# Mixer block on one core: the last query block as two half passes, closing products over 128 rows

## The chip, the cores and the metric

The kernel runs on one core of one Trainium2 chip. The metric is the device time of one execution in microseconds. Engines are named as in the profile: PE multiplies matrices (PEld are its weight loads), DVE and ACT work element by element, POOL too, and SP issues the DMAs.

## What is computed

```python
def reference(A_x, A_wqkv, A_wo, B_x, B_w1, B_b1, B_w2, B_b2):
    xn = layernorm(A_x)                              # 2048 x 640
    q, k, v = split(xn @ A_wqkv)                     # 32 heads of 20
    p = softmax(q @ k.T / sqrt(20))                  # per head, 2048 x 2048
    s = concat_heads(p @ v) @ A_wo                   # attention
    h = layernorm(xn)                                # B_x is not used
    u = gelu(h.T @ B_w1 + B_b1)                      # token MLP, 640 x 1536
    g = silu((u @ B_w2 + B_b2).T)                    # 2048 x 640
    return A_x + s * g
```

All arrays are bf16. The exponentials of the attention, 32 x 2048 x 2048 of them, are most of the work.

## The kernel before

**Passes.** The 32 heads are eight groups of four (`NG`, `GH`), the 2048 queries four blocks of 512 (`NTB`). One pass is one head group with one query block; there are 32 (`passes`, L852 to L855), and the last eight alternate between groups 6 and 7, so that group 7 with query block 3 comes last. A pass has 16 key chunks of 128. A unit is one chunk and one head: a score product of 32 rows by 128 columns with 512 queries as the moving side (`emit_st`, L1206, head g on row group 32g of the array), then exponentials, then a product P·V of 128 rows by 21 columns (20 values and a column of ones for the denominator; `pv_mm`, L1284, head g on column group 32g). All P·V products of a pass add up in PSUM bank 6 (`AB`).

**Two ways for the exponentials.** Most units go to ACT, which takes two or three PSUM banks in one instruction (L1235, 128x1024 or 128x1536). Of the chunks in `RC` some go to DVE: it makes the bit pattern of a power of two from a score (L1246), and of this tile three shifted ones (L1268, one instruction for four heads each); four P·V products with differently scaled values (`v_sb`, `vs_sb`) sum them up. Such a chunk costs DVE 4 + 3 instructions, and PE four P·V products a head.

**The order.** A planner in `schedule` writes the instruction list of every engine when the kernel is built. It keeps a modelled time for each engine and picks, step by step, among ready score groups, P·V groups, the steps of jobs, and fillers (`emit_fill`, L1299, products with zero weights that add nothing), with settings for each 16 units from a fixed table (`PLAN`, `tune`). Each engine runs its own list in order; semaphores carry the waits. In the planner, products on different groups of the array share 216 ns.

**Around the output.** When the last P·V product of a pass is placed, `ep_steps` (L1377) puts the epilogue on DVE: a transpose out of bank 6 (L1400), reciprocals of the denominators, a multiplication, and for groups 6 and 7 a transpose back into `stage_sb`. The results of groups 0 to 5 come back through DRAM into `oT_sb` (which is `xnT_sb`) as chunks 0 to 3, those of groups 6 and 7 as chunk 4. The closing product of a block of 128 queries is five products of `oT_sb` with `wo` (`op_mms`, L929), for 512 output columns and once more for the last 128; then DVE multiplies by the gate (L944) and adds x (L954). For the blocks of query block 3 chunk 4 holds only group 6, 48 rows, and L929 takes just these 48; group 7's share comes from `stage_sb` by one further product (L934).

**The tail.** Blocks 12 to 15 are closed in the tail. `tail_pre` and `tail_pre_b` (the 128-column parts of all four blocks, in bank 7, `JB`, cleared by a product with zeros, L1631) place the products with L929; the epilogue of the last pass is in two halves of 256 queries (L1392 to L1399); `tail_end` adds L934; `tail_fin` multiplies (L1607) and adds (L1609, on POOL for the first two blocks); `tail_b` does the 128-column parts at once (L1623, L1625); four stores (L1616) end it.

Of the kernel before, what the change touches and what calls it, by code (L numbers as in the profile page):

```python
# [6 lines left out]
dt = mybir.dt  # L7
# [3 lines left out]
P = 128  # L11
# [249 lines left out]
class _Kern:  # L261
# [154 lines left out]
    def schedule(self):  # L416
# [437 lines left out]
        passes += [(L6, 0), (L6, 1), (L7, 0), (L7, 1), (L6, 2), (L7, 2), (L6, 3), (L7, 3)]  # L854
        NP = len(passes)  # L855
        pass_of = {gp: q for q, gp in enumerate(passes)}
        UP = NB * GH

# [56 lines left out]

        def reload7_steps(p):
            def make(bk):
                return oT_loads(560, 640, p * 512, 512, [S_(f"oTd{L7}_{p}")], f"oTb_{p}", f"oTl7{p}") + [
                    ("tag", f"oT5_{p}")]
            return make  # L920

        def op_mms(b, ap, c0, n, bslot, first=True, last=True, opens=True, closes=True):
# [3 lines left out]
            if first:  # L926
                for c in range(5):
                    k = 128 if c < 4 or full else 48
                    steps.append(("pe", lambda e, c=c, k=k: e.matmul(  # L929
                        ap, oT_sb[0:k, c, b * 128:(b + 1) * 128], wo_ap[0:k, c, c0:c0 + n], start=(opens and c == 0),  # L930
                        stop=(full and c == 4)),
                        oT_slots.get(("oTa", c), []) + oT_slots.get((f"oTb_{p}", c), []) + [S_("wo")], [bslot], f"op{b}", mm(n)))
# [26 lines left out]
        def store_steps(p):  # L959
            def make(bk):  # L960
                dst = out[0, p * 512:(p + 1) * 512, :].rearrange("(b p) d -> p b d", p=P)
                src = regC[:, p * 4:(p + 1) * 4, :]
                return [("dma", lambda e: e.dma_start(dst, src), [S_(f"res{b}") for b in range(4 * p, 4 * p + 4)], [],
                         f"out{p}", 655360)]
            return make
# [42 lines left out]

        def activate():
            changed = True  # L1010
# [54 lines left out]
        pv_tot = [UP] * NP  # L1065
        pv_left = [UP]
# [6 lines left out]
        def chunk_ok(q, c):  # L1073
            G, p = passes[q]
            return f"qk{G}_1_{c // 4}{kpart(c) if G == 0 else ''}" in done and f"qk{G}_0_{p}" in done

        def next_chunk(q, cl):
            while q < NP:
                free = [c for c in range(NB) if (q, c) not in cl]
                if free:  # L1080
                    nr = [c for c in free if c not in RC]
# [40 lines left out]
        def a_left(q):  # L1122
            n = sum(4 for c in range(NB) if (q, c) not in claimed)
            if a_cur[1] is not None and a_cur[0] == q:
                n += GH - a_cur[2]
            return n

        done_cost = {"pe": 0.0, "dve": 0.0, "act": 0.0}
        def d_claimable():
            if not self.DON:  # L1130
                return None
            if tfree and dlive[0] < self.NLIVE:
# [3 lines left out]
                for q in (q0, q0 + 1):  # L1136
# [5 lines left out]
                    for r, c in enumerate(RC):  # L1142
# [48 lines left out]
        def emit_st(lst, banks):  # L1191
# [6 lines left out]
            for i, (q, c, g) in enumerate(lst):  # L1198
# [3 lines left out]
                lhsT = qk_sb[32 * g:32 * g + 32, slot, 1, c * 128:(c + 1) * 128]  # L1202
                rhs = qk_sb[32 * g:32 * g + 32, slot, 0, p * 512:(p + 1) * 512]
                outp = ps(bk)
                cost = (first if i == 0 else 0.0) + (20.0 if i < n - 1 else tot - 20.0 * (n - 1))
                pr.pe(lambda e, outp=outp, lhsT=lhsT, rhs=rhs, g=g: e.matmul(outp, lhsT, rhs, start=True, stop=True,  # L1206
                                                                            tile_position=(32 * g, 0)),
                      reads=[S_(f"qkb{slot}_0_{p}_{g}"), S_(kslot(slot, c, g))] + ([S_(f"qkp_{g}")] if slot else []), writes=[bank_slot[bk]],
                      name=f"st{q}_{c}_{g}", cost=cost, w=53.0)
# [70 lines left out]
        def pv_mm(q, g, lhsT, rhs, reads, cost, name, last):  # L1280
            k = pv_seen.get((q, g), 0)
            pv_seen[(q, g)] = k + 1
            outp = ps_all[32 * g:32 * g + DH + 1, AB * 512:AB * 512 + 512]
            pr.pe(lambda e: e.matmul(outp, lhsT, rhs, start=(k == 0), stop=last, tile_position=(0, 32 * g)),  # L1284
                  reads=reads, writes=[bank_slot[AB]], name=name, cost=cost, w=53.0)
# [3 lines left out]
        def fill_ok():  # L1289
            q = pv_pass[0]  # L1290
            return (acc_ok[0] and q < NP and all(pv_seen.get((q, g), 0) > 0 and pv_g_left.get((q, g), NB) > 0
                                                 for g in range(4)))

        def emit_fill():
            tot = 216.0 + pe_cost("pv", 0.0)
            for g in range(4):
                outp = ps_all[32 * g:32 * g + DH + 1, AB * 512:AB * 512 + 512]
                rhs = wp_sb[:, 0:2, :, :]
# [14 lines left out]
        def emit_pv(items, quads):  # L1313
# [22 lines left out]
            for g in range(4):  # L1336
                left = pv_g_left.get((q, g), NB) - len(ends) - sum(1 for x in items if x[1][2] == g)
# [3 lines left out]
            for i, s in enumerate(seq):  # L1341
                cost = tot / n
                if s[0] == "d":
                    _, d, k, g = s
                    c, b = d["c"], d["tl"][k]
                    if k == 0:
                        lhsT = v_sb[:, c, G * 4 + g, 0:DH + 1]
                        rd = [S_(f"v{half}_{c}")]
                    else:
                        lhsT = vs_sb[:, G % 2, k - 1, d["r"], g * 22:g * 22 + DH + 1]  # L1350
                        rd = [S_(f"vs{G % 2}_{k - 1}_{d['r']}")]
                    rhs = dt_sb[:, b, g, :].bitcast(bf)
                    pv_mm(q, g, lhsT, rhs, rd + [S_(f"dt{b}_{g}")], cost, f"pvd{q}_{c}_{g}", i in final)
                else:
# [3 lines left out]
                    pv_mm(q, g, v_sb[:, c, G * 4 + g, 0:DH + 1], pt_sb[:, s0, :], [S_(f"pt{s0}"), S_(f"v{half}_{c}")],  # L1358
                          cost, f"pv{q}_{c}_{g}", i in final)
# [7 lines left out]
            if pv_left[0] == 0:  # L1367
                pv_pass[0] += 1
                pv_left[0] = UP
# [7 lines left out]
        def ep_steps(q):  # L1377
            G, p = passes[q]
            last_pass = q == NP - 1
            s_ = q % 2  # L1380
            steps = []
            if last_pass:
                def half(h):
                    a, b = 256 * h, 8 * h
                    din = bass.AP(tr_sb, a, [[512, P], [32, 8]])
                    rd = rden_sb[:, b:b + 8]
                    nin = bass.AP(tr_sb, a + 1, [[512, P], [32, 8], [1, DH]])
                    rin = bass.AP(rden_sb, b, [[16, P], [1, 8], [0, DH]])
                    nout = bass.AP(on_sb, a + 1, [[512, P], [32, 8], [1, DH]])
                    tr, on, rs = S_(f"tr_{h}"), S_(f"on_{h}"), S_(f"rden_{h}")  # L1390
                    return (
                        ("dve", lambda e: e.transpose(tr_sb[:, a:a + 256], ps(AB, 256, a)), [bank_slot[AB]], [tr],  # L1392
                         f"eqT{h}", 366.0),
                        ("dve", lambda e: e.reciprocal(rd, din), [tr], [rs], f"eqr{h}", 110.0),
                        ("dve", lambda e: e.tensor_tensor(nout, nin, rin, ALU.mult), [tr, rs], [on], f"eqm{h}", dv(160)),
                        ("dve", lambda e: e.transpose(stage_sb[:, 2, a:a + 256], on_sb[:, b:b + 8, :].rearrange(
                            "p a b -> p (a b)")), [on], [S_(f"stage2_{h}")], f"eqb{h}", 361.0))
                A, B = half(0), half(1)
                return [A[0], A[1], B[0], A[2], B[1], A[3], ("tag", f"ep{q}_0"), B[2], B[3], ("tag", f"ep{q}_1")]  # L1399
            steps.append(("dve", lambda e: e.transpose(tr_sb[:, :], ps(AB)), [bank_slot[AB]], [S_("tr")], f"epT{q}", 632.0))  # L1400

            def okacc():
                acc_ok[0] = True
            steps.append(("call", okacc))
# [170 lines left out]
        for p in range(NTB - 1):  # L1575
            for b in range(4 * p, 4 * p + 4):
                rq = ("oT", "wo", f"oT5_{p}", f"oT4_{p}", f"x2_{p}", f"a2_{b}")
# [3 lines left out]
            add_job(f"st{p}", store_steps(p), tuple(f"res{b}" for b in range(4 * p, 4 * p + 4)), 30.0)  # L1581

        LB = [NB - 4 + i for i in range(4)]
# [10 lines left out]
        def tail_end(i):  # L1594
            b, bk = LB[i], tbank[i]
            steps = []
            if i == 2:
                for k in range(4):
                    steps += op_mms(LB[k], ps(JB, 128, 128 * k), 512, 128, bank_slot[JB], False, True, False, k == 3)
            steps += op_mms(b, ps(bk), 0, 512, bank_slot[bk], False, True)  # L1600
            steps.append(("tag", f"tend{i}"))
            return steps

        def tail_fin(i):
# [4 lines left out]
            steps.append(("pool" if i < 2 else "dve", lambda e: e.tensor_tensor(g0, g0, regA[:, b, 0:512], ALU.add),  # L1609
                          [S_(f"r{b}_0"), S_(f"x2_{NTB - 1}")], [S_(f"res{b}")], f"tr{b}a",  # L1610
                          1180.0 if i < 2 else dv(512, .52)))
# [7 lines left out]
        def tail_b():  # L1619
            gb = regC[:, NB - 4:NB, 512:640]  # L1620
            xb = regA[:, NB - 4:NB, 512:640]
            pb = ps(JB).rearrange("p (i n) -> p i n", i=4)
            return [("dve", lambda e: e.tensor_tensor(gb, pb, gb, ALU.mult),  # L1623
                     [bank_slot[JB]] + [S_(f"g{b}") for b in LB], [S_("rb")], "tpB", dp(512)),
                    ("dve", lambda e: e.tensor_tensor(gb, gb, xb, ALU.add), [S_("rb"), S_(f"x2_{NTB - 1}")],  # L1625
                     [S_("resb")], "trB", dv(512, .52)), ("tag", "tB")]

        tail_req = ("oT", "wo", f"x2_{NTB - 1}", f"oT4_{NTB - 1}") + tuple(f"a2_{b}" for b in LB)
        for i in range(4):
            add_job(f"tpre{i}", (lambda bk, i=i: tail_pre(i) + [("tag", f"tpre{i}")]), tail_req + (f"tbank{i}",), 60.0, at=NP - 1.9)  # L1630
# [3 lines left out]
        add_job("tpreb", (lambda bk: [zero] + sum((tail_pre_b(i) for i in range(4)), []) + [("tag", "tpreb")]),  # L1634
                tail_req + (f"bankoff{JB}",), 59.0, at=NP - 1.9)
        for i in range(4):
# [375 lines left out]
```

The softmax here doesn't subtract the row's maximum and nothing guards it: scores larger than these inputs give would overflow.

## Time and profile before

| what | us |
|---|---|
| median of 3 runs (lowest, highest) | 755.73 (755.54, 755.74) |
| profiled execution: from the first to the last instruction | 753.7 |
| median less span: what lies around it | 2.07 |
| last exponential starts | 740.76 |
| last P·V product starts | 742.88 |
| last closing product starts (L934) | 749.54 |
| last store is issued | 751.29 |

The profiled execution is one launch; its own time is taken as the span and the 2.07 us around it. Matmuls are shown from their start to a modelled end: a product with 512 moving columns shows 0.38 to 0.39 us even where the next starts 0.216 after it, so starts tell more than durations. DVE and ACT instructions overlap their neighbours a little too: L1246 shows 0.68 and comes every 0.60, the exponential of 1024 columns comes every 0.90 and that of 1536 every 1.33.

### The profile page before, as it was taken

The numbers are of one execution on the slowest core, as the hardware profiler recorded it, in microseconds if no ns is written. First come the engines' busy times: TensorE is split into PE (matmuls) and PEld (weight loads), VectorE is DVE, ScalarE is ACT, GpSimd is POOL, SyncE is SP. The second block draws the span as 40 slices with busy tenths as digits, with TensorE's granted clock in tenths as the row PEclk, the third lists the DMA queues.
The fourth block names the chain that finished last, engine by engine and source line by source line (L and its number), as shares of the span: only waits on it lengthen the run. The fifth ranks groups of instructions, "written<-read, shape, count | busy, mean of one in ns | idle before, by whom it ended". The sixth has DMA issues, their size and how long they took to land.

```text
span 753.7 us, 23158 instructions
## 1 busy us (share of the span) xinstructions
PE 717.6 (95%) x10302; PEld 240.7 (32%) x10302; DVE 721.0 (96%) x1320; ACT 729.9 (97%) x695; POOL 15.6 (2%) x22
## 2 busy tenths in 40 slices
PE   9999999999999999999999999999999988998997
PEld 7432223222323232323223323233333232222222
DVE  8869999999999999999999999999999999999997
ACT  4999999999999999999999999999999999999993
POOL 4200000000000000000000000000000000000001
PEclk9999999999999999999999999999999999999999
DMA  9584111110313031121014022223124340011011
GB/s 245 109 167 57 38 26 38 20 36 7 86 14 77 13 68 38 35 61 21 7 37 111 26 49 52 47 54 102 44 57 82 76 150 11 6 47 48 13 47 36
DMA packets 117143, 42.54 MB, mean 56 GB/s; under 512 B 75300, under 2 KB 115876, under 8 KB 116996
## 3 DMA queue, kind: packets, MB, share of 16 engines
q1 hardware_dynamic: 117044, 41.07, 23.9%
q8 instruction: 80, 1.31, 0.7%
q14 instruction: 19, 0.16, 0.1%
HBM read 26.37 MB, written 10.22 MB: 49 GB/s over the span
## 4 chain that ended last, share of the span: by engine, by line
ACT 85%; PE 12%; DVE 2%; DMA 1%; issue 0%; POOL 0%
ACT pt_sb L1235 83%; PE ps_all L1284 4%; PE ps_all L644 4%; PE ps_all L1206 4%; ACT zt_sb L840 1%; ACT zt_sb L835 1%; PE ps_all L929 1%; DMA xnT_sb<-regC 1%; DVE bst_sb L531 0%; DVE bst_sb L533 0%; DMA regA<-in_A_x_dram 0%; DVE regC L549 0%; DVE regC L1607 0%; PE ps_all L683 0%; DVE xnT_sb L611 0%
## 5 line engine op out<-in xcount | busy, mean ns | idle before, releaser
L1235 ACT ACTIVATE pt_sb<-ps_all 128x1024 bf16<-128x1024 f32 (+1 forms) x672 | 710.5, 1226 | 2.4 <-PE ps_all L1206 1.9
L1246 DVE TENSOR_SCALAR dt_sb<-ps_all 128x512 uint16<-128x512 f32 x496 | 328.2, 684 | 10.1 <-PE ps_all L1206 8.3
L1206 PE MATMUL ps_all<-qk_sb 32*128 32x512 bf16 x2048 | 266.7, 384 | 27.7 <-ACT pt_sb L1235 24.8
L1268 DVE TENSOR_SCALAR dt_sb<-dt_sb 128x2048 uint16<-128x2048 uint16 x372 | 241.9, 687 | 1.4
L1206 PEld LDWEIGHTS ps_all<-qk_sb 32*128 32x128 bf16 x2048 | 67.0, 91 | 283.8 <-ACT pt_sb L1235 231.8
L1284 PE MATMUL ps_all<-dt_sb,vs_sb 128*21 128x512 bf16 x1488 | 124.6, 382 | 0.8 <-DVE dt_sb L1268 0.7
L1284 PE MATMUL ps_all<-pt_sb,v_sb 128*21 128x512 bf16 x1552 | 124.2, 382 | 0.9 <-DVE tr_sb L1400 0.6
L644 PE MATMUL ps_all<-regB,regA 128*32 128x128 bf16 (+1 forms) x1536 | 68.2, 301 | 0.7 <-DVE regB L845 0.3
L644 PE MATMUL ps_all<-regC,regA 128*32 128x512 bf16 (+1 forms) x1536 | 68.4, 301 | 0.0
L1284 PE MATMUL ps_all<-dt_sb,v_sb 128*21 128x512 bf16 x496 | 49.0, 384 | 0.3 <-DVE tr_sb L1400 0.2
L644 PE MATMUL ps_all<-xnT_sb,wqk_sb 128*32 128x512 bf16 x640 | 48.2, 382 | 0.3 <-DVE zt_sb L814 0.2
L1284 PEld LDWEIGHTS ps_all<-dt_sb,vs_sb 128*21 128x21 bf16 x1488 | 31.5, 91 | 41.3 <-issue 21.9
L1284 PEld LDWEIGHTS ps_all<-pt_sb,v_sb 128*21 128x21 bf16 x1552 | 28.7, 90 | 47.7 <-issue 38.0
L644 PEld LDWEIGHTS ps_all<-regB,regA 128*32 128x32 bf16 x1536 | 27.2, 96 | 27.0 <-issue 13.1
L644 PEld LDWEIGHTS ps_all<-regC,regA 128*32 128x32 bf16 x1536 | 27.3, 96 | 25.6 <-issue 13.4
L929 PE MATMUL ps_all<-wv_sb,xnT_sb 128*128 128x128 bf16 (+3 forms) x160 | 29.5, 302 | 0.1
L644 PE MATMUL ps_all<-wv_sb,xnT_sb 128*32 128x480 bf16 x320 | 23.0, 369 | 0.0
L1400 DVE STREAM_TRANSPOSE tr_sb<-ps_all 128x512 f32<-128x512 f32 x31 | 22.1, 711 | 0.9 <-PE ps_all L1284 0.7
L644 PEld LDWEIGHTS ps_all<-xnT_sb,wqk_sb 128*32 128x32 bf16 x640 | 13.7, 95 | 18.2 <-issue 7.7
L1284 PEld LDWEIGHTS ps_all<-dt_sb,v_sb 128*21 128x21 bf16 x496 | 12.6, 90 | 21.3 <-issue 14.7
L814 DVE TENSOR_SCALAR zt_sb<-ps_all,b2h_sb 128x512 bf16<-128x512 f32 (+1 forms) x32 | 17.2, 544 | 0.0
L1044 DVE CAST v_sb<-ps_all 128x480 bf16<-128x480 f32 (+1 forms) x22 | 13.4, 610 | 3.3 <-PE ps_all L737 3.1
(82 smaller groups left out, 307.0 us busy)
## 6 DMA issues: line engine op xcount, KB each, us to landing
regA<-in_B_w_dram SPq DMA_DIRECT2D x6, 1024.0 KB
regA<-in_B_w_dram SPq DMA_DIRECT2D x8, 768.0 KB
qk_sb<-qk_scratch_dram SPq DMA_DIRECT2D x56, 80.0 KB
qk_scratch_dram<-qs_sb SPq DMA_DIRECT2D x32, 128.0 KB
regA<-in_A_x_dram SPq DMA_DIRECT2D x6, 640.0 KB
ok_scratch_dram<-on_sb SPq DMA_DIRECT2D x96, 20.0 KB
out_dram<-regC SPq DMA_DIRECT2D x3, 640.0 KB
wqk_sb<-in_A_wqkv_dram SPq DMA_DIRECT2D x2, 480.0 KB
```

The source lines that it names most:

```text
L644: fns.append(lambda e, c=c, e_=e_: e.matmul(oc(c, e_), lhsT[:, c:e_], rhs, start=start, stop=stop, tile_position=(0, c)))
L814: steps.append(("dve", lambda e, z=z, i=i, jj=jj: e.tensor_scalar(z[:, c0:c0 + n], ps(bk, n, i * n), 0.5, bias[:, jj:jj + 1], ALU.mult, AL ...
L835: steps.append(("act", lambda e: e.activation(tt_, tt_, AF.Tanh, scale=1.5957691216), [stt], [stt], f"th{j}", ac(n)))
L840: steps.append(("act", lambda e: e.activation(tt_, z, AF.Tanh), sz, [stt], f"th2_{j}", ac(n)))
L929: steps.append(("pe", lambda e, c=c, k=k: e.matmul(ap, oT_sb[0:k, c, b * 128:(b + 1) * 128], wo_ap[0:k, c, c0:c0 + n], start=(opens and c ...
L1044: return lambda e: e.tensor_copy(dst, src)
L1206: pr.pe(lambda e, outp=outp, lhsT=lhsT, rhs=rhs, g=g: e.matmul(outp, lhsT, rhs, start=True, stop=True, tile_position=(32 * g, 0)), reads=[ ...
L1235: tk = pr.act(lambda e: e.activation(outp, inp, AF.Exp, scale=math.log(2.0) / 128.0), reads=[bank_slot[b] for b in banks[:n]], writes=[S_( ...
L1246: tk = pr.dve(lambda e: e.tensor_scalar(w, src, WOFF, 0.0, ALU.add, ALU.max), reads=[bank_slot[bk]], writes=[S_(f"dt{d['tl'][0]}_{g}")], n ...
L1268: tk = pr.dve(lambda e: e.tensor_scalar(dst, src, dk, None, ALU.add), reads=[S_(f"dt{b0}_{g}") for g in range(4)], writes=[S_(f"dt{b}_{g}" ...
L1284: pr.pe(lambda e: e.matmul(outp, lhsT, rhs, start=(k == 0), stop=last, tile_position=(0, 32 * g)), reads=reads, writes=[bank_slot[AB]], na ...
L1400: steps.append(("dve", lambda e: e.transpose(tr_sb[:, :], ps(AB)), [bank_slot[AB]], [S_("tr")], f"epT{q}", 632.0))
```

## The change

The last pass, group 7 with query block 3, becomes two consecutive passes of 256 queries (`HALF`). A unit of such a pass is a pair of key chunks with one head (`HP`): two score products of 256 queries, side by side in one PSUM bank, so that ACT and DVE still see 512 columns, and two P·V products of 256 queries, one after the other into the same 256 columns of bank 6. A half pass has eight units a head instead of 16. The two chunk pairs (2, 5) and (8, 11) may go to DVE. `NP` is 33; the number of units is as before, and so is the table of settings. The planner prices each of the two products at half of what one was.

Each half pass has its own epilogue of 256 queries. Blocks 12 and 13 become ordinary closing jobs that wait for the epilogue of the first half (with the product with `stage_sb` in them), and have one store. Blocks 14 and 15 alone stay for the tail; the order of its products is changed a little, and only the first block's add is on POOL. `op_mms` always takes all 128 rows of chunk 4. For query block 3 rows 48 to 127 of it are set to zero by one DMA from a zero tile (`zero_steps`), once, after the 16 transposing loads of `oT_sb`; with it, the DMAs behind it move on by one of the eight queues' semaphores. `activate` skips a call when nothing has changed since the last, at build time only.

In the instruction lists the two kernels agree up to the first score products of the last pass, but for the zero DMA. In the last passes DVE takes one chunk less than before (from 714.2 us of the profile before on, ACT has 64 units in place of 60), and the fillers there are 20 in both, of 256 columns instead of 512 after the change. The closing products of blocks 12 and 13 stand between the P·V groups of the second half pass.

```diff
-        passes += [(L6, 0), (L6, 1), (L7, 0), (L7, 1), (L6, 2), (L7, 2), (L6, 3), (L7, 3)]
+        passes += [(L6, 0), (L6, 1), (L7, 0), (L7, 1), (L6, 2), (L7, 2), (L6, 3), (L7, 3), (L7, 3)]
...
+        HALF = {NP - 2: 0, NP - 1: 1}
+        HP = ((0, 1), (3, 4), (6, 7), (9, 10), (12, 13), (14, 15), (2, 5), (8, 11))
+        units, dunits = [], []
+        for q, (G, p) in enumerate(passes):
+            if q in HALF:
+                a = 256 * HALF[q]
+                units.append([[(c0, p * 512 + a, 256, 0, a), (c1, p * 512 + a, 256, 256, a)] for c0, c1 in HP])
+                dunits.append([(6, (0, 1)), (7, (2, 3))])
+            else:
+                units.append([[(c, p * 512, 512, 0, 0)] for c in range(NB)])
+                dunits.append([(c, (r,)) for r, c in enumerate(RC)])
...
+        def zero_steps():
+            d = oT_sb[48:128, 4, (NTB - 1) * 512:NTB * 512]
...
+            return [("dma", lambda e: e.dma_start(d, bass.AP(zw_sb, 0, [[32, 80], [0, 16], [1, 32]])), [S_("zw")], [ws],
+                     "oTz", 81920, xall), ("tag", "oTz")]
...
-                    k = 128 if c < 4 or full else 48
-                    steps.append(("pe", lambda e, c=c, k=k: e.matmul(
-                        ap, oT_sb[0:k, c, b * 128:(b + 1) * 128], wo_ap[0:k, c, c0:c0 + n], start=(opens and c == 0),
+                    steps.append(("pe", lambda e, c=c: e.matmul(
+                        ap, oT_sb[:, c, b * 128:(b + 1) * 128], wo_ap[:, c, c0:c0 + n], start=(opens and c == 0),
...
-                pr.pe(lambda e, outp=outp, lhsT=lhsT, rhs=rhs, g=g: e.matmul(outp, lhsT, rhs, start=True, stop=True,
-                                                                            tile_position=(32 * g, 0)),
...
+                np_ = len(units[q][c])
+                for ch, col, m, off, _ in units[q][c]:
+                    lhsT = qk_sb[32 * g:32 * g + 32, slot, 1, ch * 128:(ch + 1) * 128]
+                    rhs = qk_sb[32 * g:32 * g + 32, slot, 0, col:col + m]
+                    outp = ps(bk, m, off)
+                    pr.pe(lambda e, outp=outp, lhsT=lhsT, rhs=rhs, g=g: e.matmul(outp, lhsT, rhs, start=True, stop=True,
+                                                                                tile_position=(32 * g, 0)),
...
+                          writes=[bank_slot[bk]], name=f"st{q}_{c}_{g}", cost=cost / np_, w=53.0 / np_)
...
-                    pv_mm(q, g, v_sb[:, c, G * 4 + g, 0:DH + 1], pt_sb[:, s0, :], [S_(f"pt{s0}"), S_(f"v{half}_{c}")],
-                          cost, f"pv{q}_{c}_{g}", i in final)
+                    un = units[q][c]
+                    for ch, _, m, off, acol in un:
+                        pv_mm(q, g, v_sb[:, ch, G * 4 + g, 0:DH + 1], pt_sb[:, s0, off:off + m], m, acol,
+                              [S_(f"pt{s0}"), S_(f"v{half}_{ch}")], cost, f"pv{q}_{c}_{g}", i in final and ch == un[-1][0])
...
-            if last_pass:
-                def half(h):
...
-                A, B = half(0), half(1)
-                return [A[0], A[1], B[0], A[2], B[1], A[3], ("tag", f"ep{q}_0"), B[2], B[3], ("tag", f"ep{q}_1")]
...
+            if q in HALF:
+                h = HALF[q]
...
-        for p in range(NTB - 1):
-            for b in range(4 * p, 4 * p + 4):
...
+        add_job("oTz", zero_steps(), ("oT",), 40.0)
+        for p in range(NTB):
+            bs = range(4 * p, 4 * p + (4 if p < NTB - 1 else 2))
...
+                if p == NTB - 1:
+                    rq += (f"ep{NP - 2}",)
...
-        LB = [NB - 4 + i for i in range(4)]
+        NL = 2
+        LB = [NB - NL + i for i in range(NL)]
...
-            steps.append(("pool" if i < 2 else "dve", lambda e: e.tensor_tensor(g0, g0, regA[:, b, 0:512], ALU.add),
+            steps.append(("pool" if i < 1 else "dve", lambda e: e.tensor_tensor(g0, g0, regA[:, b, 0:512], ALU.add),
```

## The prediction

> **What bounds the kernel now.** I read the busy shares and the chain of work that ended last on the page, then the waits of the last stretch, the chain of its last 19 us, and single lines of the timeline.
>
> ```profile
> PE 717.6 (95%) x10302; PEld 240.7 (32%) x10302; DVE 721.0 (96%) x1320; ACT 729.9 (97%) x695; POOL 15.6 (2%) x22
> ...
> ACT 85%; PE 12%; DVE 2%; DMA 1%; issue 0%; POOL 0%
> ...
> L1235 ACT ACTIVATE pt_sb<-ps_all 128x1024 bf16<-128x1024 f32 (+1 forms) x672 | 710.5, 1226 | 2.4 <-PE ps_all L1206 1.9
> ```
>
> ACT's exponentials set the pace: 85% of the chain. PE and DVE are full too, at 95% and 96%, so PE has little room. The waits from 713.7 to 742.9 us (the last query block) say how much:
>
> ```profile
> PEld ps_all L1206 <- ACT pt_sb L1235: 9.7, 22, 0.8
> ...
> ACT pt_sb L1235 <- PE ps_all L1206: 0.5, 1, 0.5
> ```
>
> Weight loads wait 9.7 us for ACT here, but most of that overlaps matmuls still running. From the starts of the matmuls, PE is really late by only 2.8 us in these 29.2, and filler products (L1299) take some 1.1 more. A few us more on PE make PE the bound. After the last exponential the chain is serial:
>
> ```profile
> 740.72 1.62 PE ps_all L1284 x28
> 742.34 0.16 PE ps_all L929
> 742.50 0.76 PE ps_all L1284 x12
> 743.26 2.58 PE ps_all L929 x11
> ...
> 746.69 1.18 PE ps_all L929 x5
> 747.88 0.34 PE ps_all L934 x4
> ...
> 750.20 0.61 DVE regC L1607
> 750.81 0.02 issue
> 750.83 0.42 DVE regC L1609
> ```
>
> The last P·V product starts at 742.88 us; the span ends at 753.66. These 10.8 us are what the change means to shorten. PE fills most of them with closing products (L929, L934) of four blocks. How PE shares its array is read from the timeline (start, duration, engine, work):
>
> ```profile
> 44.73 0.60 PE L1206 MATMUL ps_all<-qk_sb 32*128 32x512 bf16 x6
> ...
> 199.00 1.69 PE L644 MATMUL ps_all<-regC,regA 128*32 128x128 bf16 x108
> ...
> 721.00 0.39 PE L1206 MATMUL ps_all<-qk_sb 32*128 32x512 bf16 x3
> 721.86 0.39 PE L1206 MATMUL ps_all<-qk_sb 32*128 32x512 bf16 x3 [0.47 <-ACT pt_sb L1235]
> 722.18 0.61 PE L1284 MATMUL ps_all<-pt_sb,v_sb 128*21 128x512 bf16 x8
> ```
>
> Three score products on three row groups take 0.39, as one does. Six need four groups, two of them twice: 0.60. Eight P·V products, two on each of four column groups: 0.61. So different groups run together some 3.5 ns apart, and a second product on the **same group** starts 0.216 us after the first (512 columns); with 128 columns the 108 products give (1.69-0.22)/26 = 0.056. A change of kind costs 0.10 more: 722.18 is 0.32 after 721.86.
>
> **What the Trainium skill says.** "TensorE: Matmul & The Clock Gate", Back-to-back issue gap: 518 cycles at 512 columns, 262 at 256, 134 at 128; at 2.4 GHz 0.216, 0.109, 0.056 us. The trace agrees at 512 and 128 and has no 256-column product, so I take 0.109. The same page, Part 3, The mechanism: "MATMULs are pc-monotone in start AND end", that is, none overtakes another. The trace fits this, but has no place where a product that waits for its group stands ahead of one whose group is free. "TensorEngine Tiling (Array Packing)", Key Properties: changing the tiling mode drains the array; that is the 0.10 us above. On the clock, see the second rival.
>
> **The change, part by part.** Up to the score block at 721.86 us the instruction lists of the engines agree but for the half-pass units lent to DVE (two 256-column products in place of one of 512 at the end of a triple: 0.007+0.109+0.207 = 0.323 us against 0.322) and the zero DMA. I start there.
>
> *Half passes on PE.* A unit is now two products of 256 queries, issued one after the other on the same head, so on the same row group (scores) or column group (P·V). In order, the stream runs a,a,b,b,c,c: the second a waits 0.109 for the first and holds back b, though b's group is free. A unit then takes 0.109+0.0035 = 0.1125 us. Before, four units on four groups took 0.216, or 0.054 each. After the last of a block, a change of kind comes 0.107+0.10 = 0.207 later. From 721.86 to the last P·V product the list after holds:
> - 53 score units in 16 blocks: 53 x 0.1125 + 16 x 0.207 = 9.27;
> - P·V: 112 units (48 from ACT; four DVE chunks of four heads, each with four tiles: 64) in 13 blocks: 112 x 0.1125 + 13 x 0.207 = 15.29;
> - eight P·V products of the pass before, 0.53, and 20 fillers of 256 on four groups, 5 x 0.109 + 0.10 = 0.65;
> - full-array work at 0.216 and 0.056 a product: blocks 10 and 11, then 12 and most of 13, which are new in this place: 0.38+0.97+0.32+0.38+1.18+0.32+0.44+1.40 = 5.39.
>
> Sum 31.1 us, where the list before took 742.88-721.86 = 21.0. PE is the bound then, not ACT.
>
> *Waits added.* ACT needs no more than 14 x 0.903 + 12 x 1.330 = 28.6 us from 714.24 (pitches of the timeline), to 742.8; DVE gives it one chunk more (four units, 1.7 us), hidden under PE. DVE has one chunk less, 7 x 0.60 = 4.2. Walking the lists with these prices, PE still waits 0.17 for the transpose ahead of the first P·V of the half pass, 0.23 and 0.34 for banks that ACT still reads where three score blocks stand close together, and 0.12 for the transpose of half 0: 0.86. The product with half 0's result (L934's successor) waits for DVE at the head of PE's queue with all scores behind it; DVE has it ready about 743.4 and PE comes there at 747.5, so nothing; were PE four us faster, this wait would show. Last P·V start: 721.86+31.1+0.86, less the 0.207 counted behind it: 753.7.
>
> *The tail.* Two blocks are left in place of four, and no product of 48 rows. Such a product changes the tiling twice:
>
> ```profile
> 744.48 0.09 PEld L929 LDWEIGHTS ps_all<-wv_sb,xnT_sb 48*128 48x128 bf16 x1 [0.42 <-issue]
> ...
> 744.80 0.55 PEld L929 LDWEIGHTS ps_all<-wv_sb,xnT_sb 128*128 128x128 bf16 x4 [0.23 <-issue]
> ```
>
> It comes 0.312 after its forerunner and holds its follower 0.318 back, 0.63 where two plain gaps make 0.43: 0.2 us each, four large and one small after the last P·V, 1.0 in all. After: 0.207 to the first closing product, then 5 x 0.216 + 8 x 0.056 + 0.056 + 0.216 = 1.80 to the product with the stage, which DVE (transpose, reciprocal, multiply, one 128-column product, transpose: 0.33+0.49+0.25+0.28+0.20+0.50) has ready at 2.05. Then 0.216+0.39+0.11+1.08 = 1.80 to the last product, at 3.85. From there before took 753.66-749.54 = 4.12, of which 0.09 was DVE busy with adds: 4.03. The tail is 7.9 us in place of 10.8.
>
> *Zero rows by DMA.* 80 x 16 runs of 64 bytes, 1280 packets. The page's 117044 packets took 23.9% of 16 engines' 753.7 us, 24.6 ns each, so 2.0 us of all engines and one more issue on SP, behind the 16 transposes near 598 us. Behind it stand loads that wait for PE until 607.5 and others first read at 639.0. Nothing on the path; without that cover, 0 to 2.0 us. That the lanes of later DMAs shift by one I put at 0, bounded by the 0.2 us that L929 waits for a DMA at all.
>
> Sum against the profiled span: 753.7+7.9 = 761.6, so +7.9 on 753.66. The median is 755.73, 2.07 over the span, for what lies around it; I carry that over: **763.7 us**.
>
> **The rivals.** *Pairs overlap after all* (products pass a held one, or the pair doesn't hold its group): then units cost 0.054, PE needs 31.1 less 165 x 0.0585 = 9.7, about 21.4, and ACT bounds again: its work ends at 742.8 at best, 743.5 with the 0.7 us of idleness it has before. Last P·V 0.4 later, tail 7.9, 2.07 around: 753.2 to 753.9, say 753.6, faster. For it: only the skill, no line here, says that nothing overtakes. Against: 44.73, where the same-group product waits, and that page. It decides if the stretch from 721.86 takes under about 23.9 us (21.0 plus the 2.9 of the tail): above that the change loses. Chance 0.09.
>
> *The clock drops as well.* Between 728 and 745 us about 105 units x 0.053, fillers 0.5 and 0.3 of full-array work make 6.4 us of array work in 17, or 0.37. The page's clock row never drops, but it rarely had so little work per time. The same skill page, Part 1, tells of half clock after a window of some 3.4 us without work; no run here shows where it begins. Each such window costs 1.7 us; two: 767.1. Chance 0.22.
>
> *Only the scores serialise*, column groups overlap: 112 x 0.0585 = 6.6 less, 757.1. Chance 0.06. That it doesn't shorten the tail is no case of its own: the list has two blocks there.
>
> **How the numbers follow.** Forecast 0.63, clock 0.22, scores alone 0.06, overlap 0.09. The forecast's own range is 761 to 766: the pitch may be 5 to 10 ns longer if loads don't hide (165 units, +0.8 to 1.6), the waits may be 0 to 2.5. The range 760.0 to 768.5 adds most of the clock case and leaves the two others out. What a measurement here can tell from no change is about 0.2%, 1.5 us. Faster 0.09; same 0.04 (scores alone with fewer waits); slower 0.87.
>
> **What would show it.** Score triples in the last block should take 0.61 (0.33 to the last start plus 0.28) and P·V groups of 16 about 1.17; ACT and DVE should wait for PE from 724 us on, several us in all; the last P·V should start near 753.7 and the span end 7.9 later; L929's successor should have no gap of 0.42 in the tail. I am wrong if pairs of different heads start 3.5 ns apart, if the last P·V starts before 746, or if the clock row shows a drop.

## The result and the profile after

The changed kernel takes 754.07 us (17 runs, 753.73 to 755.99), the kernel before 755.80 beside it (17 runs). The ratio is 0.9976 with a 95% interval of 0.9969 to 0.9982: 1.7 us **faster**, where 8 us slower was forecast, and outside the range. It is near what the rival "Pairs overlap after all" gave (753.2 to 753.9), which had a chance of 0.09.

The page of the kernel after, its busy shares, the chain by engine and the exponentials:

```profile
PE 712.8 (95%) x10451; PEld 243.7 (32%) x10466; DVE 718.4 (96%) x1316; ACT 731.4 (97%) x696; POOL 14.5 (2%) x21
...
ACT 84%; PE 12%; DVE 2%; DMA 1%; SPq 0%; issue 0%; ACTq 0%
...
L1271 ACT ACTIVATE pt_sb<-ps_all 128x1024 bf16<-128x1024 f32 (+1 forms) x673 | 712.2, 1227 | 1.9 <-PE ps_all L1242 1.5
```

ACT is still the pace of the kernel as a whole, with 1.5 us more busy time and 1.9 us of idleness before its exponentials in place of 2.4. PE has 4.8 us less busy time although it has more products. Two waits from 713.7 to 744.5 us:

```profile
PEld ps_all L1242 <- ACT pt_sb L1271: 7.1, 19, 0.8
DVE regC L968 <- PE ps_all L958: 3.6, 3, 1.4
```

PE's weight loads for scores wait for ACT 7.1 us (9.7 before). The forecast had ACT and DVE waiting for PE from 724 us on, several us in all: ACT has no wait for PE among the waits of this stretch, and DVE has 3.6 us, ahead of its multiplications for closed blocks. But ACT is not alone at the end. The chain that ended last runs along DVE from 723.15 to 735.65 us, and then, but for one multiplication of DVE at 742.18, along PE to the end of the P·V products:

```profile
735.28 0.37 DVE tr_sb L1436
...
735.69 1.06 PE ps_all L1320 x32
...
743.78 0.21 PE ps_all L958
744.00 0.56 PE ps_all L1320 x16
```

ACT shows no gap there either, and its last exponential ends at 743.72. So DVE, PE and ACT reach the last P·V products nearly together. The end of the timeline after (start, duration, engine, work):

```profile
740.18 0.63 PE L1320 MATMUL ps_all<-dt_sb,vs_sb 128*21 128x256 bf16 x16
740.74 0.40 PE L1242 MATMUL ps_all<-qk_sb 32*128 32x256 bf16 x6
...
743.62 0.38 PE L958 MATMUL ps_all<-wqk_sb,stage_sb 128*128 128x512 bf16 x1
743.93 0.63 PE L1320 MATMUL ps_all<-pt_sb,v_sb 128*21 128x256 bf16 x16
...
746.33 0.38 PE L958 MATMUL ps_all<-wqk_sb,stage_sb 128*128 128x512 bf16 x1
...
748.13 0.38 PE L958 MATMUL ps_all<-wqk_sb,stage_sb 128*128 128x512 bf16 x1
...
749.45 0.42 DVE L1654 TENSOR_TENSOR regC<-regC,regA 128x512 bf16<-128x512 bf16 x1
```

Six score products, three pairs each on one row group, show 0.40 in place of the forecast's 0.61; sixteen P·V products, two for each of eight units on four column groups, show 0.63 in place of 1.17. The starts of the single products, read from the traces, say how. They are offsets in us from the first of a block (before at 722.77 us; after at 739.53 and 740.18); the instruction order after is a a b b c c, that is, two products for head a, then two for b:

```
before, scores, three of 512:          0     0.003 0.006
after,  scores, a a b b c c of 256:    0     0.007 0.014   0.120 0.127 0.133
after,  P.V, a a b b c c d d of 256:   0     0.007 0.013 0.020   0.117 0.124 0.130 0.136
```

In the scores, the first three starts are 7 ns apart and then nothing starts for 0.106 us: these are the first products of a, b and c, and the second ones follow when the first are through. The trace does not name the heads, but the second of a pair cannot be among the first three: where a pair stands alone, at 732.09 us, its two products start 0.119 apart. The second a is held, as the prediction says, but b passes it.

**Where the time went.** The profiled span is 752.18 us where before it was 753.66. The last exponential starts at 742.67 (740.76 before), the last P·V product at 744.28 (742.88), and the tail from there is 7.90 us (10.78). So -2.88 of tail and +1.40 of a later last product make -1.48.

### The profile page after: what moved, and what is told of

Read it like the earlier page. It is cut to its first block, busy times and chain, and to the rows that moved or that the text cites. A ratio compares the mean times of both kernels' runs of the same rounds, so it can differ in the third digit from the quotient of the medians.

```text
span 752.2 us, 23467 instructions
## 1 busy us (share of the span) xinstructions
PE 712.8 (95%) x10451; PEld 243.7 (32%) x10466; DVE 718.4 (96%) x1316; ACT 731.4 (97%) x696; POOL 14.5 (2%) x21
## 4 chain that ended last, share of the span: by engine, by line
ACT 84%; PE 12%; DVE 2%; DMA 1%; SPq 0%; issue 0%; ACTq 0%
ACT pt_sb L1271 81%; PE ps_all L1320 4%; PE ps_all L1242 4%; PE ps_all L644 4%; ACT zt_sb L840 1%; ACT zt_sb L835 1%; DMA wqk_sb<-in_A_wqkv_dram 1%; DVE dt_sb L1282 1%; DVE dt_sb L1304 1%; PE ps_all L953 1%; SPq L480 0%; PE ps_all L737 0%; PE ps_all L629 0%; DVE regC L1652 0%; ACT L720 0%
## 5 line engine op out<-in xcount | busy, mean ns | idle before, releaser
L1282 DVE TENSOR_SCALAR dt_sb<-ps_all 128x512 uint16<-128x512 f32 x492 | 324.5, 680 | 10.4 <-PE ps_all L1242 8.5
L1242 PE MATMUL ps_all<-qk_sb 32*128 32x512 bf16 (+1 forms) x2112 | 267.3, 378 | 28.4 <-ACT pt_sb L1271 25.3
L1304 DVE TENSOR_SCALAR dt_sb<-dt_sb 128x2048 uint16<-128x2048 uint16 x369 | 239.2, 683 | 1.4
L1320 PE MATMUL ps_all<-pt_sb,v_sb 128*21 128x512 bf16 (+1 forms) x1604 | 124.9, 376 | 0.9 <-DVE tr_sb L1444 0.6
L1320 PE MATMUL ps_all<-dt_sb,vs_sb 128*21 128x512 bf16 (+1 forms) x1524 | 123.5, 375 | 0.8 <-DVE dt_sb L1304 0.7
L1320 PE MATMUL ps_all<-dt_sb,v_sb 128*21 128x512 bf16 (+1 forms) x508 | 48.5, 377 | 0.6 <-issue 0.3
L953 PE MATMUL ps_all<-wv_sb,xnT_sb 128*128 128x128 bf16 (+1 forms) x147 | 25.7, 294 | 2.0 <-issue 1.1
L968 DVE TENSOR_TENSOR regC<-ps_all,regC 128x512 bf16<-128x512 f32 (+1 forms) x28 | 13.4, 479 | 3.6 <-PE ps_all L958 3.6
```

The costliest lines, as they stand in the source:

```text
L953: steps.append(("pe", lambda e, c=c: e.matmul(ap, oT_sb[:, c, b * 128:(b + 1) * 128], wo_ap[:, c, c0:c0 + n], start=(opens and c == 0), st ...
L968: steps.append(("dve", lambda e: e.tensor_tensor(g, ps(bk, n), g, ALU.mult), [bank_slot[bk], S_(f"g{b}")], [S_(f"r{b}_{part}")], f"prod{b} ...
L1282: tk = pr.dve(lambda e: e.tensor_scalar(w, src, WOFF, 0.0, ALU.add, ALU.max), reads=[bank_slot[bk]], writes=[S_(f"dt{d['tl'][0]}_{g}")], n ...
L1304: tk = pr.dve(lambda e: e.tensor_scalar(dst, src, dk, None, ALU.add), reads=[S_(f"dt{b0}_{g}") for g in range(4)], writes=[S_(f"dt{b}_{g}" ...
```

## The experiments

**1. Firsts ahead of seconds.** After, with the products of a block in the order a b c a b c.

```diff
-                for ch, col, m, off, _ in units[q][c]:
-                    pr.pe(lambda e, ...: e.matmul(outp, lhsT, rhs, start=True, stop=True, tile_position=(32 * g, 0)), ...)
+                for j_, (ch, col, m, off, _) in enumerate(units[q][c]):
+                    prods.append((j_, i, lambda e, ...: e.matmul(...), ...))
+            for _, _, fn, rd, wr, nm, cost, w in sorted(prods, key=lambda x: x[:2]):
+                pr.pe(fn, reads=rd, writes=wr, name=nm, cost=cost, w=w)
```

> The changed kernel, but in every block of the half passes the first products of all units are issued ahead of all second ones (a, b, c, a', b', c' in place of a, a', b, b', c, c'). Theory P, a product that waits for its group is passed by products for free groups: no effect on the time, 754.1 within 0.6; in the trace the first products of a block start 3.5 ns apart, where they start 7 ns apart after the change because a held second one was taken up between each two. Theory F, nothing passes and the spacing of 7 ns has another cause: the spacing stays 7 ns, time the same. The in-order forecast on record would have had this kernel some 10 us faster than the changed one.

Measured 753.79 us, ratio to before 0.9970 [0.9958, 0.9981]; after has 0.9976 [0.9969, 0.9982]. A score block of this kernel, and the starts in it:

```profile
740.33 0.39 PE L1243 MATMUL ps_all<-qk_sb 32*128 32x256 bf16 x6
```

```
a b c a b c of 256:   0  0.003 0.007   0.119 0.123 0.126
```

The firsts are 3.5 ns apart where they were 7 in after: a held product that is passed costs its 3.5 ns of issue and no more. If b had been held behind the second a, this order would have won some 10 us over after. The 0.3 us that it does win can't be told from none; in its profiled execution the exponentials start 0.29 us earlier than after's already at 50 us, long before the half passes.

**2. Longer runs on one column group, in the kernel before.** Its P·V products issued head by head.

```diff
-                for k in range(d["pk"], d["pk"] + n_):
-                    for g in range(4):
+                for g in range(4):
+                    for k in range(d["pk"], d["pk"] + n_):
...
-            items = sorted(items, key=lambda x: (x[3], x[1][2]))
+            items = sorted(items, key=lambda x: (x[1][2], x[3]))
```

> The kernel before, all passes at 512 columns, but each block of P.V products is issued group by group: all products of head 0, then all of head 1, and so on (runs of two from ACT, runs of up to four from a DVE chunk). Theory P with a deep queue: 755.8 within 1. Theory P with room for one held product only: runs of two are free, runs of three or four hold the others back; some 60 to 240 us slower. Theory F (strict order): a block of eight takes 4 x 0.22 + 0.22 = 1.09 in place of 0.43 us, over 100 us slower in all.

Measured 772.23 us, ratio 1.0217 [1.0203, 1.0231]. None of the three times expected came, and as a time this is **inconclusive**: the planner made another plan (484 units on DVE where before has 496), and the order may put a wait for one head's tile ahead of other heads' products. Its blocks can still be read. Two of them, four and twelve products as the profile groups them, sixteen in all, four in a row on each column group:

```profile
342.65 0.43 PE L1284 MATMUL ps_all<-dt_sb,v_sb 128*21 128x512 bf16 x4 [0.24 <-DVE tr_sb L1401]
342.87 0.85 PE L1284 MATMUL ps_all<-dt_sb,vs_sb 128*21 128x512 bf16 x12
```

The four firsts start at 0, 0.013, 0.031 and 0.044 us, the four seconds at 0.223 to 0.268. So three held products in a row on one group are passed too, at some 15 ns for four issues, and the first product of the fourth head starts past nine held ones, three of each other head.

**3 and 4. The parts alone.** 3 is the kernel after with 48 rows again in the closing products of query block 3 and no zero DMA: the half passes alone.

```diff
-            return [("dma", lambda e: e.dma_start(d, bass.AP(zw_sb, 0, [[32, 80], [0, 16], [1, 32]])), ...
+            return [("tag", "oTz")]
...
+                    k = 128 if c < 4 or full else 48
-                        ap, oT_sb[:, c, b * 128:(b + 1) * 128], wo_ap[:, c, c0:c0 + n], ...
+                        ap, oT_sb[0:k, c, b * 128:(b + 1) * 128], wo_ap[0:k, c, c0:c0 + n], ...
```

> The changed kernel with half passes, but chunk 4 of query block 3 is taken with 48 rows again and without the zero DMA. Five such products (two of 512, three of 128 columns) lie behind the last P.V product. Theory: each costs 0.2 us in two changes of tiling, all on the path: 1.0 us slower than the changed kernel, 755.1. Rival: the waits for DVE in the tail hide them: 754.1 to 754.4.

4 is before with one last pass, and with 128 rows and the zero DMA: the rows alone.

```diff
-                    k = 128 if c < 4 or full else 48
...
+        add_job("oTz", zero_steps(), ("oT",), 40.0)
...
+        tail_req = ("oT", "oTz", "wo", f"x2_{NTB - 1}", f"oT4_{NTB - 1}") + tuple(f"a2_{b}" for b in LB)
```

> The kernel before, one last pass of 512 queries, with the other part of the change alone: 128 rows for chunk 4 and zero rows by DMA. Theory: four products of 512 and one of 128 columns behind the last P.V product lose 0.2 us each, 1.0 us in all: 754.8. Rival: DVE's epilogue hides some: 755.0 to 755.8. If the zero DMA costs anything, it shows here as an offset of the exponentials from about 600 us on; expected none.

Measured, with the profiled span's parts:

| kernel | us | ratio to before | last P·V starts | tail |
|---|---|---|---|---|
| before | 755.95 | 1 | 742.88 | 10.78 |
| 3: half passes, 48 rows | 755.39 | 0.9994 [0.9986, 1.0003] | 744.43 | 8.78 |
| 4: one pass, 128 rows | 754.27 | 0.9981 [0.9972, 0.9990] | 742.37 | 9.89 |
| after: both | 754.07 | 0.9976 [0.9969, 0.9982] | 744.28 | 7.90 |

Most of the gain is the **rows**. They shorten the tail by 0.89, and they do something that the prediction left out. Before has closing products of 48 rows ahead of the last scores too. The kernel before:

```profile
738.65 1.74 PE L929 MATMUL ps_all<-wv_sb,xnT_sb 128*128 128x128 bf16 x17
740.33 0.39 PE L1206 MATMUL ps_all<-qk_sb 32*128 32x512 bf16 x3
...
740.76 1.45 ACT L1235 ACTIVATE pt_sb<-ps_all 128x1536 bf16<-128x1536 f32 x1 [0.46 <-PE ps_all L1206]
```

and experiment 4:

```profile
738.77 1.11 PE L935 MATMUL ps_all<-wv_sb,xnT_sb 128*128 128x128 bf16 x17
739.82 0.39 PE L1212 MATMUL ps_all<-qk_sb 32*128 32x512 bf16 x3
```

The same 17 products take 1.74 and 1.11 us; three of them had 48 rows, at 0.21 each. ACT's last exponential waited 0.46 us for the scores behind them, and in experiment 4 it starts 0.5 earlier, and so does the last P·V product. The **half passes** alone shorten the tail by 2.0 us and let the last P·V product start 1.5 later: 0.6 us of time remain, which the measurement doesn't tell from none.

**5, 6 and 8. What holds the last P·V product.** A half pass has eight pairs of chunks, each with four heads; DVE takes 2 pairs in each half, which is all that may be lent, where it took 5 of the 16 chunks of before's last pass. ACT has the rest. Experiment 5 lends a third pair, with its scaled values in an added buffer, so 3 and 2; experiment 6 one pair in the second half, so 2 and 1; experiment 8 is 5 with the order of experiment 1.

```diff
-                dunits.append([(6, (0, 1)), (7, (2, 3))])
+                dunits.append([(5, (0, 1)), (6, (2, 3)), (7, (4, 5))])
```

> The changed kernel, with a third pair of chunks that the half passes may lend to DVE (and three small DVE operations that scale its values), so that DVE takes 3+2 chunks of the half passes where it took 2+2, and ACT has one half-pass chunk less (four heads of 512 exponentials, some 1.7 us of ACT). Theory now: ACT still sets the last P.V product, and the later end of its work is what the half passes gave back. Then the last exponential and the last P.V product start 1 to 1.7 us earlier (at 742.6 to 743.3 us in place of 744.28), and the time is 752.4 to 753.1 where the changed kernel has 754.07. Rival: PE sets the stretch (as the prediction had it), so ACT's share of the chunks does not matter: 754.1 within 0.3. Second rival: DVE becomes the last (its chunk ends later than ACT's): 754.5 or more.

```diff
-                dunits.append([(6, (0, 1)), (7, (2, 3))])
+                dunits.append([(6, (0, 1)), (7, (2, 3))][:2 - HALF[q]])
```

> The same knob turned the other way: the changed kernel, with one pair of chunks in place of two that the second half pass may lend to DVE, so 2+1 chunks in place of 2+2 and one chunk more for ACT. Theory now (ACT bounds): the last P.V product 1.3 to 1.75 us later, the time 755.3 to 755.9. Rival (PE bounds, ACT's extra chunk hidden under it): 754.1 within 0.3. If DVE were the last of the three: faster than 754.07.

> The changed kernel with the third DVE pair and with all first products of a block ahead of all second ones, together: the version that the theory would choose. If ACT bounds and the order gives its 0.3 us as well: 752.1 to 752.8. If the two gains are the same one (both only let ACT's last exponential go earlier by a fixed wait): as the third pair alone. If PE bounds: 753.8.

Measured beside before at 755.94 us:

| kernel | us | ratio to before | last exponential starts | DVE's last tile ends (L1304's) | last P·V starts | tail |
|---|---|---|---|---|---|---|
| after, DVE 2+2 | 754.07 | 0.9976 | 742.67 | 738.89 | 744.28 | 7.90 |
| 6: DVE 2+1 | 755.70 | 0.9997 [0.9989, 1.0005] | 744.95 | 733.71 | 746.68 | 7.22 |
| 5: DVE 3+2 | 757.69 | 1.0018 [1.0009, 1.0026] | 742.09 | 742.85 | 745.67 | 10.65 |
| 8: DVE 3+2, firsts first | 756.13 | 1.0003 [0.9996, 1.0011] | 740.23 | 742.53 | 742.84 | 10.91 |

(The intervals of 5, 6 and 8 are those of one comparison, that of after is its own.) The starts of the table are those of one execution each, and these are shifted as a whole against one another from the first 50 us on: at 700 us the exponentials stand 0.29 us later than in before for after, 0.53 later for 6, and 0.17 and 0.06 earlier for 5 and 8.

Experiment 6 took the time expected: one pair more on ACT (four units) costs 1.6 us, so ACT's share is **not** hidden. Its last P·V product comes later than expected (2.4 us, 2.2 without the shift, for 1.3 to 1.75), and its tail is shorter, with 9 closing products behind the last P·V in place of 29. The chain of waits of experiment 6 goes back to ACT's exponentials, which release five closing products that stand ahead of the last P·V block:

```profile
739.67 5.43 ACT pt_sb L1271 x4
745.09 0.05 issue
745.14 1.25 PE ps_all L953 x5
746.39 0.60 PE ps_all L1320 x16
```

Experiments 5 and 8 **missed**: the theory "ACT alone sets it" promised 752 to 753. What came is nearer to the second rival of experiment 5, that DVE becomes the last. Of experiment 8 the theory got the first half right: the last exponential is 2.4 us earlier (2.1 without the shift) and the last P·V product 1.4 (1.1). But this product now takes a tile from DVE, 0.3 us after DVE finished it, and the tail is 3.0 us longer. The timeline of experiment 8:

```profile
738.51 0.43 DVE L1457 STREAM_TRANSPOSE stage_sb<-on_sb 128x256 bf16<-128x256 bf16 x1
738.87 3.66 DVE L1315 TENSOR_SCALAR dt_sb<-dt_sb 128x2048 uint16<-128x2048 uint16 x6
...
742.72 0.39 PE L1331 MATMUL ps_all<-dt_sb,vs_sb 128*21 128x256 bf16 x8
743.05 0.39 PE L966 MATMUL ps_all<-wqk_sb,stage_sb 128*128 128x512 bf16 x1
...
743.27 1.52 PE L961 MATMUL ps_all<-wv_sb,xnT_sb 128*128 128x512 bf16 x10
743.54 0.65 DVE L976 TENSOR_TENSOR regC<-ps_all,regC 128x512 bf16<-128x512 f32 x1
```

Half 0's result is in `stage_sb` at 738.9, as in after (738.3), but its first product (L966) is placed at 743.05; in after it comes at 739.87. DVE is at its shifted tiles until 742.5 and takes its first multiplication for a closed block of query block 3 at 743.54 (740.29 in after). So the closing of blocks 12 and 13 goes behind the last P·V product: 43 closing products stand there (35 of L961, 8 of L966), 29 in after. That DVE has no time for these multiplications earlier is read from the timeline; a planner that placed the same work in another order was not tried.

Experiment 5 loses 1.6 us more than 8. The windows of its profiled execution (engine time in each stretch, then granted clock, DMA share and GB/s) show most of the cause:

```profile
733.00:737.00 4.00, 3.11 (x56) 1.04 (x54) 3.74 (x8) 4.00 (x5) 0.00 (x0) 0.96 0.28 96
737.00:741.00 4.00, 3.56 (x56) 1.85 (x60) 4.00 (x11) 3.29 (x4) 0.00 (x0) 0.50 0.01 4
741.00:745.00 4.00, 4.00 (x75) 1.73 (x65) 1.85 (x4) 1.62 (x2) 0.00 (x0) 0.69 0.00 0
```

and a score block in them:

```profile
737.22 0.61 PE L1250 MATMUL ps_all<-qk_sb 32*128 32x256 bf16 x6 [0.24 <-ACT pt_sb L1279]
```

The granted clock fell to 0.50 for some 6.8 us (0.96, 0.50 and 0.69 in three windows of 4 us), and the block of six shows 0.61 in place of 0.40. So the row of experiment 5 in the table is that of an execution with the lower clock. It is not the rule: of its 22 executions, 12 had a mean granted clock of 0.998 or less and took 757.3 to 760.3 us, and the other 10 have a median of 756.4, only 0.4 above experiment 8's of the same kind (756.0).

This is the mechanism of the rival "The clock drops as well", but not an effect of the change: the profiled execution of after keeps 1.00 in all its windows from 700 us to the end, three of after's 17 had a mean of 0.995 to 0.998 (755.2 to 756.0 us), and so had 9 of before's 59 in this comparison (0.995, 757.2 to 758.2 us). PE ran 56 products in 733 to 737 us of experiment 5 and 72 in the same window of experiment 8, which kept its clock; that this difference decides is not shown, and why experiment 5 has such executions more often stays open.

**7. How far the passing goes.** After, with each score product of the half passes split into four of 64 queries: eight in a row on one row group, the same arithmetic.

```diff
-                for ch, col, m, off, _ in units[q][c]:
+                for ch, col, m, off in [(ch, col + o, m, off + o) for ch, col, m_, off, _ in units[q][c]
+                                        for m in (64 if m_ == 256 else m_,) for o in range(0, m_, m)]:
```

> The changed kernel, with each 256-query score product of the half passes split into four of 64 queries, so that eight products in a row stand on one row group. It asks how far the passing goes. If products for a free group pass any number of held ones, a block of three heads takes about one head's eight products, 8 x 0.03 = 0.24 us plus 0.25 to the end, and only the issue of 24 products at 3.5 ns (0.08 us) is added: the firsts of three heads start some 28 ns apart, and the time is 754 to 755. If passing reaches over one held product only (the changed kernel shows no more), the heads serialise nearly fully: 24 x 0.03 = 0.72 us a block, 0.4 to 0.5 us longer in each of some 40 blocks less the slack of PE, so 765 to 775. If it reaches over some few (a queue of about four): firsts some 0.12 us apart, 758 to 764.

Measured 757.26 us, ratio 1.0015 [1.0009, 1.0022]. A block of three heads:

```profile
728.67 0.67 PE L1243 MATMUL ps_all<-qk_sb 32*128 32x64 bf16 x24
```

Its starts, sorted into heads by their steps of 0.029 us:

```
a:  0      0.039  0.068  0.097  0.126  0.155  0.184  0.214
b:  0.134  0.173  0.202  0.231  0.260  0.289  0.319  0.348
c:  0.269  0.308  0.337  0.366  0.395  0.424  0.454  0.483
```

b starts 8 ns after the fifth a, when three a's are left, and c 0.135 later in the same way. So a product passes **up to three** held ones of a group, and waits behind a fourth; experiment 2 shows that three of each of three groups can be passed. Why it ends there is not shown. That is the case "some few" of the expectation (0.12 apart was expected). The block's starts take 0.483 us, between some 0.27 for free passing (0.21 for one head and 3.5 ns for each of the 16 issues ahead of the third) and 0.70 for none (24 x 0.029). The last P·V product starts at 747.56, 3.28 after that of after, and the tail is 7.91; the time is 0.7 us below the range expected for this case.

## Why the prediction was wrong

**The step that failed** is in "Half passes on PE": "In order, the stream runs a,a,b,b,c,c: the second a waits 0.109 for the first and holds back b, though b's group is free." It does wait (0.109 to 0.121 in the starts), and it doesn't hold back b. A unit therefore costs 0.054 us as before, and 165 units x 0.0585 = 9.7 us of the sum never existed. Without them the prediction's own 31.1 + 0.86, less the 0.207 counted behind it, becomes 22.1 (with them, the last P·V product at 753.6, which the prediction rounded up to 753.7); the trace shows 744.28 - 721.86 = 22.4, of which 0.29 is the later start told below. That the rest fits so closely is partly luck: the walk put all of PE's waits at 0.86, and PE shows 1.5 us of waiting for ACT ahead of scores in this stretch alone, so some of its work was priced too high. The prediction named the missing piece of evidence itself (no place in the trace before where a product held for its group stands ahead of one whose group is free) and gave the overlap 0.09; it leaned on the Trainium skill, "TensorE: Matmul & The Clock Gate", Part 3, whose "MATMULs are pc-monotone in start AND end" the starts here contradict. On a case that the trace does not show, one sentence carried most of the chance.

**"Hidden under PE"**, ACT's one chunk more (1.7 us), fell with it. The rival had it at the right place: ACT's work ends "743.5 with the 0.7 us of idleness"; the trace has 743.72, of which 0.29 is a later start of everything (0.24 of it is there at 50 us). What the rival mis-sized is "Last P·V 0.4 later": the last P·V product starts 0.67 us after the end of the last exponential before and 0.56 after, so it should have been moved about as far as that end (742.21 to 743.72); it moved 1.40. In after the last P·V block also starts right behind a closing product on PE (743.62 and 743.93), so the trace does not say which of the two held it. Experiment 6 shows the price of four more units: 1.6 us.

**Right:** the tail. 7.9 us were forecast in place of 10.8, and 7.90 came; inside it the product with the stage (2.05 after the last P·V product: 746.33), the last closing product (3.85: 748.13) and the end (4.03 after that: 4.05). The zero DMA cost nothing: ACT's lag behind the kernel before is the same 0.29 before and after 598 us. The product with half 0's result did not wait for DVE although PE came 7.6 us earlier than forecast (739.87); the prediction expected a wait in that case, but DVE was 5 us earlier too (738.3 for 743.4).

**Mis-sized:** the 48 rows. The price of 0.2 us a product holds (0.21). Counted were the five behind the last P·V product (1.0; experiment 4: 0.89); not counted were three small ones ahead of the last scores, which held ACT's last exponential by 0.5. Experiment 3 lost 1.3 us to after where 1.0 was expected, 0.88 of it in the tail. The rows are worth 1.7 us of time in experiment 4 (755.95 to 754.27), with an interval of 0.8 to 2.1.

**The large gain that stayed small.** Half passes take 2.0 us off the tail and give 1.5 back, because fewer chunks can be lent to DVE and ACT ends later. Lending more (experiments 5 and 8) gives the end of the exponentials back in experiment 8, makes DVE the last, and pushes the closing work of blocks 12 and 13 behind the last P·V product, for 3.0 us. No run here beats after by more than the measurement tells: experiment 1 is nominally the fastest, at 753.79.

## What to carry to other kernels

Before charging matmuls for standing in line, ask which array group each needs and how many held ones of one group stand ahead of it: here up to three were passed at 3.5 ns each, and the charge for order was 9.7 us too much. When the last wave of work is cut finer to shorten a tail, count what the cut takes from each engine that shares that wave, since here one chunk more on ACT went with a last P·V product 1.5 us later, against 2.0 us won in the tail (experiment 3). And price a slow product in every place where it stands ahead of the last work of the pacing engine, not in the tail alone.

## What the runs showed of the hardware

- A product that waits for its row or column group does not hold back later products for free groups, as long as no more than three of one group are held: starts 7 ns apart past one held product (after), about 15 ns apart past three (experiment 2). Where eight stood in a row on one row group, the next head's first started 0.134 us after the first of the eight, when three were left (experiment 7).
- 256-column products on one group follow each other after 0.109 to 0.121 us, 64-column ones after 0.029 (0.039 after the first).
- A closing product with 48 rows among such with 128 cost 0.21 us (before and experiment 4: 17 products in 1.74 and 1.11 us, three of them with 48 rows).
- The granted clock fell to 0.50 for 6.8 us in the profiled execution of experiment 5. Single executions of before and after, too, had a mean granted clock of 0.998 or less and took about 1.5 us longer (before 757.4 for 755.9 in the median); what sets it off stays open.
